# Float64 weights become float32 by one whole-number addition: a change to the conversion and to the order of the first steps of a two-layer float32 kernel

## The chip, the cores and the metric

One NeuronCore of a Trainium2 chip runs the kernel. The metric is the device time of one execution in microseconds, the median of several runs.

## What is computed

```python
def _attn_ref(x, state):                       # x (4, 8, 512, 64), state (4, 8, 32, 64)
    a = softmax(x @ state.T / 8);  xread = a @ state
    a2 = softmax(state @ x.T / 8); sread = a2 @ x
    return np.concatenate([xread, sread], axis=2)

x = attn_out.transpose(0, 2, 1, 3).reshape(4 * 544, 512)   # 2176 tokens
x = (x @ w_a) * (x @ w_b) @ w_out                          # w_a, w_b (512, 1536), w_out (1536, 512)
h = x @ w_in                                               # w_in (512, 2048)
out = (np.maximum(h, 0) + np.log1p(np.exp(-np.abs(h)))) @ w_out2   # w_out2 (2048, 512)
```

(The three lines on the softmax are shortened: the reference subtracts the row's largest score and adds 1e-9 to the sum.) x and state are float32. The five weight matrices are float64, and so are the arithmetic of the last three lines' inputs: each weight arrives in memory as two 32-bit words, low and high.

## The kernel before, in words

**Weights.** A weight unit is loaded as 32-bit words (`load`, `load_first`) and made into float32 on the chip by `convert_to` (line 607). There are 32 units of 128 x 1024 values, which `convert` and `fetch` handle, and four half-units of 128 x 512 (`bring_first`), the two column halves of the first 256 columns of w_a and of w_b, which the start needs. `convert_to` takes six steps on a unit: an activation on ACT that turns the high word, read as a float32, into the upper part with its exponent moved by 2^-112 (helper line 483); a shift by three bits on DVE (line 504); the sign put back (line 508); an AND that keeps sign and exponent (line 504); the low word times 2^-52 times that (line 508); and the float addition of both (line 498).

**Products.** Most products are exact float32 products made of three products of rounded (fp32r) operands. `split_to` (line 577) makes the two operands: a copy to the rounded type, which the planner gives to ACT or DVE (lines 490, 491), and the subtraction of the rest on DVE (line 498). `Products.one` (line 545) issues one product and `turn` (line 560) a transpose on PE.

**Stages.** The first layer is worked in six stages of 256 columns (w_a and w_b) by four batches b. For the first stage the reading of the state is not projected token by token: `state_w` projects the state through w_a and w_b, and the gates are products of attention weights with that. In later stages the same is done by `state_rows` (stage s, half p): it splits a weight unit, makes twelve products of 64 state rows with 512 columns into two pairs of PSUM banks, splits each pair by `split_to`, and copies the rows into place by eight 128 KB DMAs. `gates_of` multiplies the two gate halves, `y_part` multiplies them by w_out and adds up on DVE, `read_x` and `read_y` do the same for the state's own tokens. The second layer follows, with `softplus` between its two products.

**The order.** Nothing runs when the code says it; the code lists steps in a `Plan` with the engines that can do each. `ORDER` (lines 157 to 189) gives the rank of the first 771 steps by number, the rest follows in the program's order. `Plan.go` then walks a modelled time, gives each free engine the ready step of the lowest rank, and takes storage for its results: 36 slots of 128 x 512 in SF, 58 in SR (plus x's own tiles, xf and xr, when x has been used), and 8 PSUM banks of 512 columns. So the table decides the order of the instructions on each engine's queue, and semaphores do the rest. In the first 60 us of its modelled time it puts products of zeros on PE where PE would stand still (line 572).

Of the kernel before, what the change touches and what calls it, by code (L numbers as in the profile page):

```python
# [12 lines left out]
AF = mybir.ActivationFunctionType  # L13
ALU = mybir.AluOpType
# [105 lines left out]
def made(x):  # L120
    return x.ap() if isinstance(x, Ref) else x
# [32 lines left out]


ORDER = """
1 0 3-4 6 18 5 7 17 30 10 19 13 29 20 8 31 22 9 32 21 33 12 23 214 34 11 24 215 14 35 59 25
# [4 lines left out]
118 104 146 106 173 185 147 107 186 119 183 174 236 120 184 190 175 233 121 187 122-123 237  # L162
176 188 150 189 124 158 234 258 191 259 125 247 177-178 162 159 179 192 163 193 260 160 248
261 194 149 151 238 168 165 195 161 264 219 196 201 249 164 218 166 105 240 152 197 167 265
154 182 180 155 153 235 198 220 304 250 181 170 199 171 227 207 262 200 202 239 251 290-291
263 335 252-254 242 228 241 208 221 306 203 307 224 204 223 209 222 225 293 305 210 243 205
255 206 169 244 256 309 266 308 245 294 232 336 211 267 310 229 257 270 311 337 268-269 230
212 246 296 275 213 297 322 321 338 271 226 312 272-274 339 298 276-277 313 315 340 379 314
278 284 341 299 350 316-318 343 300 319-320 279 380 342 371 351 302 324 468 280 325 285 292
301 281 344-345 352 148 372 282 353 469 373 303 382 295 358 286 381 354 374 287 357 327 385  # L170
288 329 355 386 328 470 331 347 383 356 360 346 384 330 323 471 417 333 361 363 387 348 472
366 375 473 407-408 231 401 364 477 367 289 326 332 349 475 418 283 334 376 410 402 478 474
404 359 362 476 498 479-482 365 483 409 405 499 377 388 411 368 378 415 500 462 369 505 403
370 501 406 392 446 433 432 502 506 389 412 438 390 413 439 503 419 393 414 395 435-436 396
441 463 391 504 586 464 442 434 587 448 536 588 449 537 440 451 423 443 420 428 397 444 421
589 445 590 422 452 429 465 579 425 437 484 430 416 485 595 585 431 487 591 596 399 398 488
507 426 454-455 394 427 450 447 457 453 594 490 400 597 491 424 466 510-511 494 512-513
598-599 516-518 458 519 493 526 486 527 529 467 530 523 600 524 520 489 460 508 534 461 509
495 538 496 616 541-543 615 514 497 547 551 532 580 593 552 521 554 456 581 555 622 539 560
617 563 561 531 557 565 623 558 568 533 569 571 573 572 574 583 525 540 546 515 618 566 582  # L180
703 556 492 619 528 559 553 522 562 535 575 459 564 620 545 621 592 601-602 548 604-605
607-608 577 610-611 640 567 576 584 570 654 578 549 544 550 704-705 629 609 733 624 603 606
627-628 630 709 706-707 634-635 651 637-638 708 612-613 643-644 625 646-647 614 712 669 626
641 653 713 671 642 658-661 668 714 655 664-667 645 672 639 715 675 674 677 734 633 678 716
710 631 735 682-683 686 685 739 691 688-689 649 717 692-693 696 648 632 656 736 699 676
701-702 680 650 670 737-738 657 770 652 711 694-695 662-663 673 679 718-732 697 684 681 687
636 740 690 698 741-769 700
"""


# [206 lines left out]
def attention_moe_moe2(ctx, tc, x, state, w_a, w_b, w_out, w_in, w_out2, out):  # L397
# [23 lines left out]
    scale = 1.0 / float(D) ** 0.5  # L421
# [58 lines left out]
    def activation(o, i, func, **kw):  # L480
        also = [v for v in kw.values() if isinstance(v, Ref)]
        acc = [kw["accum_out"]] if "accum_out" in kw else []
        give = lambda: nc.scalar.activation(  # L483
            made(o), made(i), func, **{k: made(v) for k, v in kw.items()})
        plan.add({"act": (act_us(cols(o), in_psum(i)), give)}, [i, *also], [o, *acc])
# [121 lines left out]
    def convert_to(v, b, spare=0):  # L607

        words = b.rearrange("p a b -> p (a b)").bitcast(U32)
        words = words.rearrange("p (c t) -> p c t", t=2)  # L610
        low, high = words[:, :, 0], words[:, :, 1]
        e = Buf(F, v.n, spare)
        v_, e_ = (i.rearrange("p a b -> p (a b)") for i in (v, e.all()))
        vu, eu = v_.bitcast(U32), e_.bitcast(U32)
        activation(v_, high.bitcast(F32), AF.Copy, scale=2.0 ** -112)
        ts(vu, vu, 3, ALU.logical_shift_left)
        stt(vu, high, 0x80000000, vu, ALU.bitwise_and, ALU.bitwise_or)
        ts(eu, vu, 0xFF800000, ALU.bitwise_and)
        stt(e_, low, 2.0 ** -52, e_, ALU.mult, ALU.mult)
        tt(v_, v_, e_, ALU.add)  # L620


    RAW_SPARE = 10
# [735 lines left out]
```

## Time and profile before

| | before |
|---|---|
| median of 3 runs | 735.59 us (735.43 to 736.33) |
| profiled execution: its own time | 734.75 us |
| its span, first to last instruction | 733.0 us |
| mean granted TensorE clock | 0.999 |
| PE busy, matmuls | 726.5 us, 99% |
| PE weight loads (beside the matmuls) | 602.4 us, 82% |
| DVE busy | 608.2 us, 83%, 810 instructions |
| ACT busy | 398.8 us, 54%, 643 instructions |
| HBM read and written | 40.11 MB and 4.46 MB |

The busy time of PE covers pipelined products, each of which starts before the one before it has ended, so a full PE starts a product of 512 columns about every quarter of a microsecond, while one product lasts 0.39 us by itself. DVE and ACT work one instruction after another. In the views "idle before" names what ended the time in which an engine stood still.

### The profile page before, as it was taken

To read this page: it belongs to the slowest core of one execution; us is meant where nothing else is said; L and a number is where in the kernel's file an instruction comes from. 1 tells how busy PE (TensorE), PEld (TensorE's weight loads), DVE (VectorE), ACT (ScalarE), POOL (GpSimd) and SP (SyncE) were. 2 spreads that over 40 slices of the span, in tenths; PEclk is the share of its full clock that TensorE was granted. 3 is DMA by queue.
4 is the path that set the end of the run, shared out by engine and by line. 5 is a ranking of instruction groups with operands and counts; after the bars stand their busy time and mean duration, and the time that the engine had idled before them with its cause. 6 is when DMAs were issued, how large, how long until landed. Compare 5 with 4: busy or idle time off the path is not lost.

```text
span 733.0 us, 10298 instructions
## 1 busy us (share of the span) xinstructions
PE 726.5 (99%) x4090; PEld 602.4 (82%) x4090; DVE 608.2 (83%) x810; ACT 398.8 (54%) x643; POOL 0.7 (0%) x6
## 2 busy tenths in 40 slices
PE   9999999999999999999999999999999999999998
PEld 8577887778888877888888898888988889888897
DVE  7999999999597779799998778569887998886574
ACT  6878655234142323235685676654766657655570
POOL 0000000000000000000000000000000000000000
PEclk9999999999999999999999999999999999999999
DMA  9403791864546356733030001001020110101103
GB/s 308 168 1 130 214 242 48 210 172 107 145 114 173 73 158 149 197 114 116 1 114 1 1 0 59 1 0 58 1 93 24 58 31 28 59 0 59 58 1 129
DMA packets 35379, 66.20 MB, mean 90 GB/s; under 512 B 3716, under 2 KB 10116, under 8 KB 35332
## 3 DMA queue, kind: packets, MB, share of 16 engines
q1 hardware_dynamic: 35332, 65.55, 30.9%
q8 instruction: 32, 0.52, 0.3%
q14 instruction: 15, 0.12, 0.1%
HBM read 40.11 MB, written 4.46 MB: 61 GB/s over the span
## 4 chain that ended last, share of the span: by engine, by line
PE 95%; DVE 2%; ACT 2%; DMA 1%; issue 0%; SPq 0%; ACTq 0%
PE PS L545 93%; PE PS L560 2%; ACT SF L490 1%; ACT SF L483 1%; DVE SF L508 1%; DMA SF<-in_moe_w_a 1%; DVE SR L498 0%; DVE SF L498 0%; DVE SF L504 0%; DVE SM L514 0%; ACT SR L490 0%; SPq L525 0%; DVE SM L519 0%; DVE SM L504 0%; DVE SF L491 0%
## 5 line engine op out<-in xcount | busy, mean ns | idle before, releaser
L545 PE MATMUL PS<-SR 128*128 128x512 f32 (+3 forms) x2187 | 534.5, 377 | 1.2 <-DVE SR L662 1.2
L545 PEld LDWEIGHTS PS<-SR 128*128 128x128 f32 (+1 forms) x2187 | 386.2, 189 | 72.1 <-issue 2.2
L483 ACT ACTIVATE SF<-SF 128x512 f32<-128x512 f32 (+3 forms) x258 | 159.2, 629 | 23.9 <-DMA SF<-in_moe_w_b 10.6
L545 PE MATMUL PS<-SR,xr 128*128 128x512 f32 (+3 forms) x473 | 147.7, 386 | 0.0
L545 PE MATMUL PS<-xr,SR 128*128 128x512 f32 (+1 forms) x378 | 133.1, 391 | 0.0
L490 ACT CAST SR<-SF 128x1024 fp32r<-128x1024 f32 (+4 forms) x97 | 74.6, 772 | 106.4 <-DVE SF L498 104.8
L498 DVE TENSOR_TENSOR SF<-SF,PS 128x1024 f32<-128x1024 f32 (+3 forms) x118 | 108.7, 931 | 26.3 <-PE PS L545 25.5
L508 DVE SCALAR_TENSOR_TENSOR SF<-SF 128x512 f32<-128x512 f32 (+6 forms) x128 | 106.4, 834 | 0.8
L545 PEld LDWEIGHTS PS<-SR,xr 128*128 128x128 f32 x473 | 88.2, 188 | 18.2 <-issue 0.7
L498 DVE TENSOR_TENSOR SR<-SF,SR 128x1024 fp32r<-128x1024 f32 (+4 forms) x96 | 82.2, 862 | 16.1 <-ACT SR L490 15.5
L490 ACT COPY SF<-PS 128x1024 f32<-128x1024 f32 (+3 forms) x88 | 55.5, 663 | 56.4 <-PE PS L545 50.8
L545 PEld LDWEIGHTS PS<-xr,SR 128*128 128x128 f32 (+1 forms) x378 | 68.6, 187 | 15.1 <-issue 0.7
L508 DVE SCALAR_TENSOR_TENSOR SF<-PS,SF 128x512 f32<-128x512 f32 (+2 forms) x74 | 45.1, 609 | 43.1 <-ACT SF L483 43.0
L498 DVE TENSOR_TENSOR SF<-SF 128x512 f32<-128x512 f32 (+3 forms) x103 | 78.2, 761 | 1.6
L483 ACT ACTIVATE SF<-PS 128x512 f32<-128x512 f32 (+2 forms) x78 | 41.5, 532 | 39.7 <-PE PS L545 38.4
L504 DVE TENSOR_SCALAR SF<-SF 128x1024 uint32<-128x1024 uint32 (+1 forms) x61 | 39.4, 652 | 5.8 <-ACT SF L483 5.4
L545 PE MATMUL PS<-SF 64*32 64x128 f32 (+4 forms) x512 | 32.4, 321 | 1.5 <-issue 0.7
L490 ACT CAST SR<-PS 128x1024 fp32r<-128x1024 f32 (+2 forms) x27 | 22.9, 864 | 20.1 <-PE PS L545 11.2
L490 ACT CAST xr<-SF 128x1024 fp32r<-128x1024 f32 (+3 forms) x26 | 20.1, 772 | 25.0 <-DVE SF L498 24.9
L498 DVE TENSOR_TENSOR SR<-PS,SR 128x1024 fp32r<-128x1024 f32 (+2 forms) x29 | 30.1, 1043 | 1.6 <-ACT SR L490 1.3
L545 PEld LDWEIGHTS PS<-SF 64*32 64x32 f32 (+2 forms) x512 | 19.8, 127 | 10.0 <-issue 7.5
L545 PE MATMUL PS<-xr,xr 128*128 128x512 f32 x56 | 22.0, 396 | 0.0
(65 smaller groups left out, 292.1 us busy)
## 6 DMA issues: line engine op xcount, KB each, us to landing
SR<-SR SPq DMA_DIRECT2D x116, 128.0 KB, 2.4
SF<-in_moe_w_out SPq DMA_DIRECT2D x11, 1024.0 KB, 5.0
SF<-in_moe_w_in SPq DMA_DIRECT2D x7, 1024.0 KB, 5.2
SF<-in_moe_w_a SPq DMA_DIRECT2D x11, 512.0 KB, 4.6
SF<-in_moe_w_b SPq DMA_DIRECT2D x11, 512.0 KB, 6.1
xr<-SR SPq DMA_DIRECT2D x36, 128.0 KB, 2.4
x<-in_x SPq DMA_DIRECT2D x8, 512.0 KB, 9.1
out<-SF SPq DMA_DIRECT2D x14, 256.0 KB, 2.2
```

The lines of the kernel that those rows point to most:

```text
L483: give = lambda: nc.scalar.activation(made(o), made(i), func, **{k: made(v) for k, v in kw.items()})
L490: "act": (act_us(n, ps), lambda: nc.scalar.copy(made(o), made(i))),
L498: put = lambda eng: lambda: eng.tensor_tensor(out=made(o), in0=made(a), in1=made(b), op=op)
L504: give = lambda: nc.vector.tensor_scalar(made(o), made(i), s1, None, op0=op0)
L508: give = lambda: nc.vector.scalar_tensor_tensor(out=made(o), in0=made(a), scalar=s, in1=made(b), op0=op0, op1=op1)
L545: self.all.append(lambda: nc.tensor.matmul(made(o), made(w), made(x), start=first, stop=last, **kw))
L560: self.all.append(lambda: nc.tensor.transpose(made(o), made(i), ident))
```

## The change

`convert_to` has five steps instead of six. The upper part is made as before. The low word is multiplied by 2^-29 on ACT and written as a whole number, which rounds it to the bits that the float32 has room for; a 32-bit whole-number addition on DVE adds it to the bits of the upper part. The AND and the product with 2^-52 are gone. `ORDER` is listed anew and covers 1921 steps instead of 771. The helper that issues products of zeros is unchanged.

```diff
 ORDER = """
-1 0 3-4 6 18 5 7 17 30 10 19 13 29 20 8 31 22 9 32 21 33 12 23 214 34 11 24 215 14 35 59 25
...
+0 3-4 6-7 5 1-2 10 8 17 13 9 18-19 29 12 20 11 30 21 31 22 32 207 33 25 23 208 58 34 24 16
...
         activation(v_, high.bitcast(F32), AF.Copy, scale=2.0 ** -112)
+        activation(eu, low, AF.Copy, scale=2.0 ** -29)
         ts(vu, vu, 3, ALU.logical_shift_left)
         stt(vu, high, 0x80000000, vu, ALU.bitwise_and, ALU.bitwise_or)
-        ts(eu, vu, 0xFF800000, ALU.bitwise_and)
-        stt(e_, low, 2.0 ** -52, e_, ALU.mult, ALU.mult)
-        tt(v_, v_, e_, ALU.add)
+        tt(vu, vu, eu, ALU.add)
```

All in all DVE's queue has 55 instructions fewer than before, ACT's 19 more, and PE's 8 fewer, all of them products of zeros. The numbers of lines in the changed kernel lie three higher from `Plan` to `convert_to` (line 545 is 548 there, 498 is 501).

In the rows of the order that follow, PS is PSUM, SR and SF are the two storages, xr_... is x's storage used as SR, and [waits ...] names the engines or DMA queues whose semaphores an instruction waits for.

PE, before: the second of the two blocks of `state_rows` of stage 3 (twelve products, in two lots of six that wait for DVE) stands between products of other work. The first block stands 108 products ahead.

```order
L545 MATMUL PS<-xr_1021,SR 128x512
L545 MATMUL PS<-SR 128x512 x2
L545 MATMUL PS<-xr_1021,SR 128x512
L545 MATMUL PS<-SR 128x512
L545 MATMUL PS<-SR 128x512 [waits DVE_49]
L545 MATMUL PS<-SR 128x512 x5
L545 MATMUL PS<-SR 128x512 [waits DVE_49]
L545 MATMUL PS<-SR 128x512 x5
L545 MATMUL PS<-xr_1021,SR 128x512
L545 MATMUL PS<-SR 128x512
```

PE, with the change: the second half of the first block, the six products of `read_y`, two turns of `read_x`, and the second block, whose halves wait for DVE each.

```order
L548 MATMUL PS<-SR 128x512 [waits DVE_49]
L548 MATMUL PS<-SR 128x512 x5
L548 MATMUL PS<-SR,xr_921 128x512 [waits DVE_49]
L548 MATMUL PS<-xr_880,xr_921 128x512
L548 MATMUL PS<-SR,xr_921 128x512 x2
L548 MATMUL PS<-xr_880,xr_921 128x512
L548 MATMUL PS<-SR,xr_921 128x512
L563 MATMUL PS<-ident,SF 128x128 [waits DMAHW5_49]
L563 MATMUL PS<-ident,SF 128x128
L548 MATMUL PS<-SR 128x512 [waits DVE_49]
L548 MATMUL PS<-SR 128x512 x5
L548 MATMUL PS<-SR 128x512 [waits DVE_49]
```

ACT, with the change, at the same place: the copies of bank pairs to rounded form. The first waits for PE, the second for DVE.

```order
L486 ACTIVATE xf<-SF 128x1024 [waits DMAHW7_49]
L493 CAST SR<-SF 128x1024 [waits DVE_49,PE_49]
L493 CAST SR<-PS 128x1024 [waits PE_49]
L493 CAST SR<-PS 128x1024 [waits DMAHW1_49,DMAHW0_49,DMAHW2_49,DVE_49,Activation_49]
L493 CAST xr_921<-PS 128x256 [waits DVE_49,PE_49]
```

The blocks moved together: about a hundred products stood between them, and eight do now.

DVE, before, at the second block of stage 4: the steps of a conversion and the evictions of banks take turns. On PE eighteen full products stand between that block and the next that waits for one of its banks.

```order
L504 TENSOR_SCALAR SF<-SF 128x1024 [waits Activation_49]
L508 SCALAR_TENSOR_TENSOR SF<-SF 128x1024 [waits DMAHW1_49,DMAHW0_49,DVE_49]
L498 TENSOR_TENSOR SF<-SF,PS 128x1024 [waits PE_49]
L504 TENSOR_SCALAR SF<-SF 128x1024 [waits DVE_49]
L498 TENSOR_TENSOR SR<-PS,SR 128x1024 [waits DMAHW5_49,DMAHW4_49,DMAHW6_49,DMAHW3_49,DMAHW7_49,DMAHW2_49,Activation_49]
L508 SCALAR_TENSOR_TENSOR SF<-SF 128x1024 [waits DVE_49]
L498 TENSOR_TENSOR SR<-PS,SR 128x1024 [waits DMAHW6_49,DMAHW5_49,DMAHW7_49,DMAHW4_49,Activation_49]
```

DVE, with the change, at the first block of stage 4: additions that wait for PE's y products, one conversion of a unit to its end (ISA is the whole-number addition), then the subtractions that free two pairs of banks.

```order
L501 TENSOR_TENSOR SF<-SF,PS 128x1024 [waits PE_49] x4
L507 TENSOR_SCALAR xf<-xf 128x1024 [waits Activation_49]
L511 SCALAR_TENSOR_TENSOR xf<-SF,xf 128x1024 [waits DMAHW7_49,DVE_49]
L501 ISA xf<-xf 128x2048 [waits DVE_49]
L501 TENSOR_TENSOR SR<-PS,SR 128x1024 [waits DMAHW6_49,DMAHW1_49,DMAHW7_49,DMAHW0_49,Activation_49]
L501 TENSOR_TENSOR SR<-PS,SR 128x1024 [waits DMAHW4_49,DMAHW3_49,DMAHW5_49,DMAHW2_49,Activation_49]
```

PE, with the change, there: the last of the y products, the block, and three lots of gate products; the last three wait for the first of those subtractions.

```order
L548 MATMUL PS<-xr_956,xr_880 128x512
L548 MATMUL PS<-SR 128x512 [waits DVE_49]
L548 MATMUL PS<-SR 128x512 x5
L548 MATMUL PS<-SR 128x512 [waits DVE_49]
L548 MATMUL PS<-SR 128x512 x5
L548 MATMUL PS<-SR 128x512 [waits DMAHW1_49,DMAHW0_49,DVE_49]
L548 MATMUL PS<-SR 128x512 x2
L548 MATMUL PS<-SR,xr_921 128x512 [waits DMAHW6_49,DMAHW7_49,DMAHW3_49,DMAHW2_49]
L548 MATMUL PS<-SR,xr_921 128x512 x2
L548 MATMUL PS<-SR,xr_880 128x512 [waits DVE_49]
```

The evictions moved behind a whole conversion, and the products that want their banks moved up: six full products stand between the block and the one that waits.

At the second block of stage 4 DVE now has these rows: its own copy of a bank pair waits for PE's last y product, and an addition and the subtraction follow. On PE the two turns and the block stand right behind that y product, and the block's second half and the gates after it wait for DVE.

```order
L501 TENSOR_TENSOR SF<-SF,PS 128x1024 [waits PE_49] x2
L494 CAST xr_880<-PS 128x1024 [waits PE_49]
L501 TENSOR_TENSOR SF<-SF,PS 128x1024
L501 TENSOR_TENSOR xr_880<-PS,xr_880 128x1024 [waits DVE_49]
L501 TENSOR_TENSOR xr_921<-PS,xr_921 128x256 [waits Activation_49]
```

The rows of before for this block are those of DVE above: the copy was made on ACT there, and the block came 114 products later.

## Rows read from the trace of the kernel before

**Rows 1.** The page: busy time of each engine, and the chain that ended last.
```profile
PE 726.5 (99%) x4090; PEld 602.4 (82%) x4090; DVE 608.2 (83%) x810; ACT 398.8 (54%) x643; POOL 0.7 (0%) x6
...
PE 95%; DVE 2%; ACT 2%; DMA 1%; issue 0%; SPq 0%; ACTq 0%
```

**Rows 2.** Waits of PE: total us, times, longest us; the first three rows.
```profile
PE PS L545 <- DVE SR L662: 1.2, 1, 1.2
PE PS L545 <- issue: 0.7, 1, 0.7
PE PS L545 <- DVE SR L498: 0.5, 1, 0.5
```

**Rows 3.** Windows: length; busy us of PE, PEld, DVE, ACT, POOL; clock; DMA share; GB/s.
```profile
20.00:40.00 20.00, 18.36 (x266) 12.47 (x265) 19.25 (x31) 15.13 (x26) 0.00 (x0) 1.00 0.35 120
40.00:60.00 20.00, 19.90 (x183) 13.44 (x182) 19.84 (x25) 17.32 (x30) 0.00 (x0) 1.00 0.05 9
150.00:250.00 100.00, 100.00 (x461) 80.76 (x460) 82.46 (x80) 33.27 (x35) 0.00 (x0) 1.00 0.55 137
```

**Rows 4.** Groups by line and shape, conversion steps: busy us, mean ns; idle before.
```profile
L483 ACT ACTIVATE SF<-SF 128x512 f32<-128x512 f32 x145 | 91.5, 634 | 5.9 <-DMA SF<-in_moe_w_a 1.0 <-DVE SF L498 0.6 <-DMA SF<-in_moe_w_b 0.5
...
L504 DVE TENSOR_SCALAR SF<-SF 128x1024 uint32<-128x1024 uint32 x53 | 36.1, 687 | 3.9 <-ACT SF L483 3.6
...
L498 DVE TENSOR_TENSOR SF<-SF 128x1024 f32<-128x1024 f32 x25 | 30.5, 1219 | 0.2
L483 ACT ACTIVATE SF<-SF 128x1024 f32<-128x1024 f32 x26 | 29.5, 1136 | 16.6 <-DMA SF<-in_moe_w_b 10.1 <-DMA SF<-in_moe_w_out 6.5
...
L508 DVE SCALAR_TENSOR_TENSOR SF<-SF 128x1024 f32<-128x1024 uint32 x23 | 28.1, 1223 | 0.4
L508 DVE SCALAR_TENSOR_TENSOR SF<-SF 128x1024 uint32<-128x1024 uint32 x23 | 28.1, 1223 | 0.3
```

**Rows 5.** Timeline of DVE, first conversion: start us, length us, instruction.
```profile
6.87 0.43 DVE L504 TENSOR_SCALAR SF<-SF 128x512 uint32<-128x512 uint32 x1
7.34 0.69 DVE L508 SCALAR_TENSOR_TENSOR SF<-SF 128x512 f32<-128x512 uint32 x1
8.06 0.69 DVE L498 TENSOR_TENSOR SF<-SF 128x512 f32<-128x512 f32 x1
```

**Rows 6.** Timeline of PE from 19.61 us; idle time before in brackets.
```profile
19.61 1.97 PE L560 MATMUL PS<-ident,x 128*128 128x128 f32 x16
21.97 0.66 PE L560 MATMUL PS<-ident,SF 128*128 128x128 f32 x4 [0.39 <-ACT SF L490]
22.38 0.71 PE L572 MATMUL PS<-SR 128*128 128x256 f32 x4
23.02 1.44 PE L545 MATMUL PS<-SF 64*32 64x128 f32 x64
...
27.45 0.69 PE L545 MATMUL PS<-SF 64*32 64x128 f32 x29 [0.50 <-DVE SR L498]
28.88 3.62 PE L545 MATMUL PS<-SF 64*32 64x128 f32 x41 [0.74 <-issue]
```

**Rows 7.** The chain that ended last: start us, length us, what.
```profile
63.90 9.55 PE PS L545 x42
```

**Rows 8.** Groups by line and shape, evictions of PSUM: columns as in rows 4.
```profile
L498 DVE TENSOR_TENSOR SF<-SF,PS 128x1024 f32<-128x1024 f32 x59 | 71.6, 1216 | 16.9 <-PE PS L545 16.5
...
L498 DVE TENSOR_TENSOR SR<-PS,SR 128x1024 fp32r<-128x1024 f32 x21 | 25.4, 1218 | 1.3 <-ACT SR L490 1.3
...
L490 ACT CAST SR<-PS 128x1024 fp32r<-128x1024 f32 x19 | 18.9, 1016 | 15.6 <-PE PS L545 10.4 <-DMA xr<-SR 2.2 <-PE PS L560 1.6
```

**Rows 9.** Timeline of PE at a block of `state_rows`, stage 4.
```profile
202.80 0.38 PE L560 MATMUL PS<-ident,SF 128*128 128x128 f32 x2
203.11 1.65 PE L545 MATMUL PS<-SR 64*128 64x512 f32 x12
204.69 0.97 PE L545 MATMUL PS<-SR,xr 128*128 128x512 f32 x3
```

More of the change, by code (lines that the diff above doesn't have):

```diff
@@ L156 @@
 ORDER = """
-1 0 3-4 6 18 5 7 17 30 10 19 13 29 20 8 31 22 9 32 21 33 12 23 214 34 11 24 215 14 35 59 25
[4 rows of a table removed]
[L162 to L184, printed above, removed]
@@ L185 @@
-710 631 735 682-683 686 685 739 691 688-689 649 717 692-693 696 648 632 656 736 699 676
-701-702 680 650 670 737-738 657 770 652 711 694-695 662-663 673 679 718-732 697 684 681 687
-636 740 690 698 741-769 700
+0 3-4 6-7 5 1-2 10 8 17 13 9 18-19 29 12 20 11 30 21 31 22 32 207 33 25 23 208 58 34 24 16
+209 59 128 60 36 35 210 129 61 38 26 130 63 62 37 14 67 39 15 28 40 70 27 41 76 71 43 78 87
+45-46 42 64 123 44 47 66 88 80 77 48 124 131-132 68 134 85 121 50 133 54 51 49 86 73 135 122
[3 rows of a table added]
+252 143 154 182 230 155 183 169 253 226 188 119 254 170 227 211 189 171-173 240 156 120 212
@@ new lines @@
+158 241 144 157 297 257 174 147 159 148 242 255 258 160 298 201 256 101 149 162 192 244 163
+150 176 243 175 259 231 161 245-247 299-300 193 228 195-196 194 233 164-165 260 232 262 202
+328 197 261 301 198-199 236 204 203 302 234-235 200 205 264 213 268 206 263 284 237-238 329
+214 331 283 269 265-267 286 220 215 342 248 216 221 249 239 287 330 223 303 217 315 289 250
+290 332 218 304 343 314 344 291 270 333 305 273 224 285 345 271 292 306-307 274 222 219 309
+293 317 288 308 277 370 279 334 310 346 318 311-312 225 336 335 280 347 272 313 362 364 363
@@ new lines @@
+275 278 376 294 316 371 320 295-296 349 373 324 348 339 374 321 338 351-352 281 337 354 375
+322 357-358 372 487 323 325 486 488-489 355 319 408 490 397 466 398 365 400 327 367 458 407
+391 276 467 392 468 377 405 394-395 340 378 469-470 341 359 401 471 492 459 462 366 572 326
+573 436 461 423 452 460 356 368 523 360 350 369 353 463 574 524 361 399 493 402 393 379 491
+382 403 422 282 381 575 429 380 406 426 577 580 464 385 576 396 453 581 428 454 386-387 409
+582 600 388 583 430 425 437 584 431 585 424 383 432 413 404 601 384 439 410 438 419 434 441
@@ new lines @@
+389 411-412 606 498 455 566 442 435 418 433 607 472 416 473 475-476 390 494 415 521 427 478
[4 rows of a table added]
+552 529 551 571 561 535 696 559 589-590 579 694 592-593 595 562 530 587 608 563 638 531 537
+588 613 564 596 609 556 611-612 614 594 565 557 618-619 624 635 621 560 610 692 627-628 695
+630-631 597 615 653 591 625 598 616 655 632 642-645 622 599 652 648-651 629 656 623 636 659
+639 658 661 717 617 662 555 693 715 718 666-667 670 669 720 675 672-673 633 586 676-677 680
+626 640 716 683 660 685 699 664 634 654 719 641 751 554 687 678-679 646-647 657 663 700-714
@@ L188 @@
+681 668 665 671 620 721 674 682 722-750 684 752-801 803-804 802 805-823 825-826 824 827-851
+853-854 852 855-877 879-880 878 881-966 968-969 967 970-1186 1188-1189 1187 1190-1230
+1232-1233 1231 1234-1247 1249-1250 1248 1251-1283 1285-1286 1284 1287-1503 1505-1506 1504
+1507-1547 1549-1550 1548 1551-1564 1566-1567 1565 1568-1600 1602-1603 1601 1604-1820
+1822-1823 1821 1824-1864 1866-1867 1865 1868-1881 1883-1884 1882 1885-1917 1919-1920 1918
 """
```

11 rows, old and new, of the table ORDER are left out of this document.

## Prediction

> **What bounds the kernel now.** I read the page's busy times and its chain first, then TensorE's waits, then the windows, then the timeline of the places that the change touches. TensorE (PE) is busy for 726.5 of the 733.0 us of the span, and the chain that ended last is 95% PE [rows 1]. PE's list of waits, sorted by size, begins with 1.2 us for the first zeros at the very start, and goes on with 0.7 and 0.5 us [rows 2]. Between 150 and 250 us PE has no idle time at all, 100.00 of 100.00. Only the first 60 us leave something: 18.36 of 20 and 19.90 of 20 us, in the windows from 20 to 60 [rows 3]. So work taken from VectorE (DVE) or given to ScalarE (ACT) is worth nothing by its sum. It is worth what it does to the first 60 us, and what it does to the moment at which a PSUM bank that PE wants comes free.
>
> **Part 1, the six steps that become five.** For a unit of 1024 columns the AND (0.687 us) and the product with 2^-52 (1.223 us) go, and the float addition (1.219 us) becomes a whole-number addition; for a unit of 512 columns 0.43 and 0.69 us go [rows 4, 5]. There are 32 units of the first kind and four of the second: 32 x 1.91 + 4 x 1.12 = 65.6 us less on DVE. ACT gets one more activation per unit, 1.136 or 0.634 us [rows 4]: 32 x 1.136 + 4 x 0.634 = 38.9 us. ACT is busy 54% of the span and DVE 83% [rows 1]; both lie beside a PE that is full, so both sums go into the result as nothing. The cover is the distance between a unit's load and its first product. Where it ends, it ends in a wait for a bank, and those are in part 3.
>
> The whole-number addition has no row. The instruction order shows it as one instruction over 2048 columns for a unit of 1024 words, so over 16-bit halves. From below: 0.687 us, the row of a 1024-column step with one input [rows 4]. From above: if it goes through 2048 columns at the pace of the float addition, which takes 0.69 us for 512 [rows 5] and 1.219 for 1024 [rows 4], that is 1.219 + 2 x 0.53 = 2.28 us. I take 1.22 us, the float addition's row, because it reads two inputs and moves the same number of bytes. The Trainium skill, page "VectorE: DVE Perf Modes", section "The perf-mode tier table", puts a 16-bit tensor_tensor over 2,048 columns at 1224 ns and a 4-byte float one at 2293 ns: by the first figure the sum here stays as it is, by the second it is that of the third rival below. No row here shows either.
>
> **Part 2, the start.** The first conversion runs on DVE without a gap: the steps that go are the AND, at 6.87 us, and the product with 2^-52, at 7.34 us; the addition follows at 8.06 us [rows 5]. Four of these half-units lie one behind the other before the first gate products, which need the state projections of all four. Four times 1.12 us is 4.5 us of DVE. PE cannot use all of it, since the last of x that the start needs lands at 19.7 us whatever DVE does: PE's turns of x begin at 19.61 us and run without a wait [rows 6]. After them PE waits 0.39, 0.50 and 0.74 us, and fills 0.64 us (22.38 to 23.02) with zero products [rows 6]. That is 2.27 us which a DVE that is 4.5 us further on can give back. From below it is nothing, if the waits only move to the next turn; from above 2.4 us, the 1.74 us that PE is idle from 20 to 60 us [rows 3] and the 0.64 us of zero products. I take **2.0 us gained**, near the top, as DVE's relief is twice what PE can use. Eight zero products fewer are issued in the whole program; they only stand in waits and give nothing of their own. In SyncE's queue the second half of w_b moves from the ninth to the eighth load, and the second half of x's third batch is the eleventh in both, so the landing that holds PE at 19.6 us is not moved.
>
> **Part 3, the three waits that come.** The list of first steps is new, and in it the blocks that project the state rows through the next stage's weights (twelve products of 64 rows) stand closer together and closer to other products. A block takes two pairs of banks of the four pairs there are, and a pair is free only when its values are copied to rounded form and subtracted (the copy takes 1.016 us on ACT, and on DVE as I take it 1.22, like the addition from PSUM; the subtraction 1.218 on DVE [rows 8]). PE's side of each sum uses 0.227 us per full product (9.55 us for 42 [rows 7]), 1.58 us for a block (203.11 to 204.69) and 0.31 us for two turns (202.80 to 203.11) [rows 9].
>
> *Stage 3, near 159 us.* Before, its two blocks stand 108 products apart. Now six products and two turns lie between them. ACT's first copy waits for PE, because it writes into slots that the first block still reads. From the end of that block: copy 1.02, subtract 1.22, then the next copy 1.02 and subtract 1.22, since the second copy waits for DVE: 4.48 us until the second pair of banks is free. PE has six products (1.36), two turns (0.31) and half of the second block (0.79) to do meanwhile: 2.46. PE waits **2.0 us** in two pieces. If ACT's first copy could start before the block ends, 1.0 us less.
>
> *Stage 4, first block, near 188 us.* The bank that the second group of gate products wants belongs to an older pair, and its subtraction now stands on DVE behind an addition that waits for the end of PE's y products, a shift, a sign step and the whole-number addition of one weight unit. From the end of the y products: 1.22 + 0.69 + 1.22 + 1.22 + 1.22 = 5.57 us [rows 4, 8]. PE has the block (1.58) and six products (1.36): 2.94. PE waits **2.6 us**, or 2.1 if the whole-number addition takes 0.69 us. Behind the waiting subtraction stand another subtraction and the split of a weight unit, which come later by as much as PE does.
>
> *Stage 4, second block, near 214 us.* DVE itself makes a rounded copy that waits for PE's last y product, and behind it stand an addition and the subtraction. Each of the last two frees a bank pair that PE wants: 1.22 + 1.22 + 1.22 = 3.66 us. PE has two turns and the block, 0.31 + 1.58 = 1.89. PE waits **1.8 us**. Before, this block comes over 100 products later, and eighteen full products lie between it and the first that wants one of its banks.
>
> **The sum.** -2.0 + 2.0 + 2.6 + 1.8 = +4.4 us. It stands against the profiled execution, 734.75 us: 739.2 us. The median of the runs lies 0.84 us above that execution (735.59), so I expect 740.0 us as the median. The ends: with the start at -2.4 and the waits at 4.4 us in all (stage 3 with 1.0, the whole-number addition at 0.69 us, half a us off the last) it is 737.6. With no gain in the start and 8.5 us of waits (each subtraction late by another 0.7 us, as some of them also wait for 128 KB copies of state rows) it is 744.1.
>
> **The rivals.**
> *Faster: the banks come free in time.* Then only the start is left: 734.75 - 2.0 + 0.84 = 733.6 us. For it speaks that DVE has 66 us less to do, and that before the largest wait of PE for DVE, the first zeros apart, is 0.5 us [rows 2]. Against it, the queues of DVE and ACT are served in the order shown, and each of the three chains begins at an event of PE, so that being early elsewhere doesn't shorten it. It decides if each chain is about 2 us shorter than I count. Chance 0.12.
> *No change.* The start gives 2.4 us, and the waits come to about as much, since two of the three are covered: within 1.5 us of 735.6. Chance 0.08.
> *Slower still: the whole-number addition takes 2.28 us.* Its price is 1.06 us per unit and 0.53 per half-unit. The start loses 4 x 0.53 = 2.1 us of what it gained, and the wait near 188 us grows by 1.06: 740.0 + 2.1 + 1.06 = 743.2 us at least. The other 31 units would add up to 33 us on DVE, of which a part would reach PE; I put this case at 745 or more. It is also the case in which the addition isn't the cheap step that the change counts on. Chance 0.06.
>
> **How the numbers follow.** The forecast, three new waits that outweigh the start, has 0.74; its own range is 737.6 to 744.1, and its time is 740.0. A change under 0.2% (1.5 us) is about what a measurement of this kernel can't tell from none. Faster is the first rival, 0.12; same is the second, 0.08; slower is the forecast and the third, 0.80. The range goes from 736.0 to 744.1: below it stays the first rival, above it most of the third, under 0.2 together.
>
> **What would show it.** In the profile of the changed kernel, the stretch of PE that begins at 28.88 us [rows 6] should begin near 26.9. PE's waits should have three new places: about 2 us near 159, 2.6 near 188 and 1.8 near 214 us, each put down to DVE. The windows from 150 to 250 us should have 6 us of idle PE, and after 300 us nothing should change. The whole-number addition should show 1.2 us, DVE some 543 us busy and ACT some 438. I am wrong if PE is busy throughout from 150 to 250 us (first rival), or if the addition's row shows 2.3 us (third).

## The result, and the profile after

The changed kernel takes 742.3 us, the median of six runs (740.72 to 744.86). The kernel before took 735.51 us (735.31 to 736.33), measured beside it. The ratio is 1.0094, with an interval from 1.0073 to 1.0115, so the change made the kernel slower by nearly 7 us. The forecast was 740.0 us, with a range from 736.0 to 744.1. The profiled execution took 741.0 us. Its span is 739.1 us, which is 6.1 us more than before.

The page, and after it the first rows of PE's waits, answer to [rows 1, 2]. Line numbers are three higher than before, behind `convert_to` two.

```profile
PE 727.4 (98%) x4082; PEld 602.3 (81%) x4082; DVE 561.9 (76%) x755; ACT 422.1 (57%) x662; POOL 0.7 (0%) x6
...
PE 91%; DMA 4%; DVE 3%; ACT 1%; issue 0%; SPq 0%; ACTq 0%
```

```profile
PE PS L548 <- DVE SR L501: 3.8, 4, 2.4
PE PS L548 <- DVE SF L501: 1.3, 1, 1.3
PE PS L548 <- DVE SR L664: 1.2, 1, 1.2
PE PS L548 <- issue: 1.1, 1, 1.1
PE PS L563 <- DVE SF L511: 1.0, 1, 1.0
```

DVE is busy for 46 us less and ACT for 23 us more, and the kernel is slower. The list of waits says why: PE's longest wait for DVE, the first zeros apart, was 0.5 us before and is 2.4 us now.

The windows (columns as in [rows 3]) show where PE stands idle.

```profile
20.00:40.00 20.00, 18.86 (x284) 13.48 (x269) 19.09 (x31) 19.71 (x33) 0.00 (x0) 1.00 0.34 119
40.00:60.00 20.00, 20.00 (x205) 13.89 (x206) 19.69 (x25) 17.18 (x30) 0.00 (x0) 1.00 0.19 64
...
150.00:200.00 50.00, 46.50 (x215) 35.88 (x214) 29.51 (x29) 17.00 (x18) 0.00 (x0) 1.00 0.40 105
200.00:250.00 50.00, 48.50 (x219) 39.31 (x218) 34.31 (x33) 17.05 (x18) 0.00 (x0) 1.00 0.66 153
```

From 150 to 250 us PE had no idle time before; now it has 3.50 + 1.50 = 5.0 us. The timelines of PE and DVE at the first block of stage 4 show the longest wait as it arises. The columns are start, length, instruction, and in brackets the idle time before it.

```profile
187.70 2.55 PE L548 MATMUL PS<-SR 64*128 64x512 f32 x15
190.08 0.85 PE L548 MATMUL PS<-SR,xr 128*128 128x512 f32 x3
193.34 0.97 PE L548 MATMUL PS<-SR,xr 128*128 128x512 f32 x3 [2.40 <-DVE SR L501]
```

```profile
187.81 1.22 DVE L501 TENSOR_TENSOR SF<-SF,PS 128x1024 f32<-128x1024 f32 x1 [1.50 <-PE PS L548]
188.95 0.69 DVE L507 TENSOR_SCALAR xf<-xf 128x1024 uint32<-128x1024 uint32 x1
189.67 1.23 DVE L511 SCALAR_TENSOR_TENSOR xf<-SF,xf 128x1024 uint32<-128x1024 uint32 x1
190.93 1.22 DVE L501 CUSTOM_DVE_ANT_0 xf<-xf 128x2048 uint16<-128x2048 uint16 x1
192.07 2.35 DVE L501 TENSOR_TENSOR SR<-PS,SR 128x1024 fp32r<-128x1024 f32 x2
```

The first of the two subtractions in the last row frees the bank that the products at 193.34 want. It comes after an addition that waited for PE and after the last three steps of one conversion. Nothing in those three steps concerns PE at that moment.

**Where the 6.1 us are.** The same work is compared, not the same time. A block of state rows begins at 124.68 us before and at 125.19 us now, but six more full products stand ahead of it now (6 x 0.227 = 1.36 us). So the start gained 0.85 us. A later block, of stage 5, has the same useful products ahead of it in both and begins at 270.93 and at 276.38, 5.45 us later; the stretch between the two blocks therefore lost 6.3 us. The last product of the program is 6.10 us later, so another 0.65 us was lost after that. In sum: -0.85 + 6.3 + 0.65 = 6.1. These are single executions: in the first two kernels below that move steps of stage 4 and share this start, the block of state rows begins at 125.17 and 125.60 us, so the 0.85 has some 0.4 us of play.

### The profile page after: what moved, and what is told of

The parts are those of the page before. It is cut to its first block, busy times and chain, and to the rows that moved or that the text cites. A ratio compares the mean times of both kernels' runs of the same rounds, so it can differ in the third digit from the quotient of the medians.

```text
span 739.1 us, 10278 instructions
## 1 busy us (share of the span) xinstructions
PE 727.4 (98%) x4082; PEld 602.3 (81%) x4082; DVE 561.9 (76%) x755; ACT 422.1 (57%) x662; POOL 0.7 (0%) x6
## 4 chain that ended last, share of the span: by engine, by line
PE 91%; DMA 4%; DVE 3%; ACT 1%; issue 0%; SPq 0%; ACTq 0%
PE PS L548 89%; DMA SF<-in_moe_w_b 2%; PE PS L563 2%; DMA SR<-SR 1%; DVE SR L501 1%; DMA SF<-in_moe_w_a 1%; DVE SF L501 1%; ACT SF L493 0%; DVE SM L517 0%; ACT SF L486 0%; DVE SR L494 0%; DVE SF L494 0%; SPq L528 0%; DVE SF L511 0%; DVE xr L501 0%
## 5 line engine op out<-in xcount | busy, mean ns | idle before, releaser
L548 PE MATMUL PS<-SR 128*128 128x512 f32 (+3 forms) x1980 | 489.9, 379 | 4.2 <-DVE SR L501 1.4
L548 PEld LDWEIGHTS PS<-SR 128*128 128x128 f32 (+1 forms) x1980 | 348.2, 189 | 72.6 <-issue 2.9
L548 PE MATMUL PS<-SR,xr 128*128 128x512 f32 (+2 forms) x580 | 165.4, 379 | 2.4 <-DVE SR L501 2.4
L548 PE MATMUL PS<-xr,SR 128*128 128x512 f32 (+2 forms) x452 | 151.3, 388 | 0.0
L486 ACT ACTIVATE SF<-SF 128x512 f32<-128x512 f32 (+5 forms) x191 | 135.4, 725 | 20.9 <-DMA SF<-in_moe_w_b 10.3
L548 PEld LDWEIGHTS PS<-SR,xr 128*128 128x128 f32 x580 | 106.4, 188 | 23.1 <-DVE SR L501 2.8
L511 DVE SCALAR_TENSOR_TENSOR SF<-SF 128x1024 uint32<-128x1024 uint32 (+4 forms) x61 | 52.4, 859 | 0.3
L501 DVE CUSTOM_DVE_ANT_0 SF<-SF 128x2048 uint16<-128x2048 uint16 (+1 forms) x33 | 38.1, 1155 | 1.6
L486 ACT ACTIVATE SF<-xf 128x512 f32<-128x512 f32 (+4 forms) x53 | 34.8, 662 | 5.6 <-DMA xf<-in_moe_w_out 4.6
L548 PE MATMUL PS<-SF 64*32 64x128 f32 (+4 forms) x512 | 32.2, 321 | 1.1 <-issue 1.1
L486 ACT ACTIVATE xf<-SF 128x512 f32<-128x512 f32 (+4 forms) x46 | 29.6, 648 | 3.1 <-DMA SF<-in_moe_w_out 1.3
```

The source lines that it names most:

```text
L486: give = lambda: nc.scalar.activation(made(o), made(i), func, **{k: made(v) for k, v in kw.items()})
L501: put = lambda eng: lambda: eng.tensor_tensor(out=made(o), in0=made(a), in1=made(b), op=op)
L511: give = lambda: nc.vector.scalar_tensor_tensor(out=made(o), in0=made(a), scalar=s, in1=made(b), op0=op0, op1=op1)
L548: self.all.append(lambda: nc.tensor.matmul(made(o), made(w), made(x), start=first, stop=last, **kw))
```

## The experiments

Nine kernels were run. The medians of the kernel before, run beside them, lie between 735.45 and 735.94 us. My theory was that a few evictions that stand behind other work on DVE's queue cost the time, and that the arithmetic of the conversion costs none. The first rival was that the new list of steps is to blame as a whole, the second that the conversion is.

**One half of the change alone.** The table `ORDER` and the steps of `convert_to` can be exchanged separately, if the numbers in a list are carried over to the same steps. The first kernel has the new conversion with the old list:

```diff
 ORDER = """
-0 3-4 6-7 5 1-2 10 8 17 13 9 18-19 29 12 20 11 30 21 31 22 32 207 33 25 23 208 58 34 24 16
+1 0 3-4 6 18 5 7 17 31 10 19 13 29 20 8 32 22 9 30 21 12 23 207 33 11 24 208 14 34 58 25 60
...
```

> The new conversion, with the list of first steps of the kernel before (each step keeps its place; the activation of the low word takes the place of the AND, the product with 2^-52 is dropped). Theory, the list makes the loss: the waits of 2.4 us near 191 us and 1.3 near 218 us are gone, PE's idle time from 150 to 250 us is under 1.5 us, and the time is 735 to 738 us. Rival, the conversion itself makes the loss (39 us more on ACT, the whole-number addition in a chain): the time stays at 740 to 743 us, whatever the order.

It took 740.33 us (739.29 to 741.58; ratio 1.0068, 1.0053 to 1.0083), about 2 us less than the changed kernel. The two long waits were gone and PE was idle for 1.46 us from 150 to 250 us, as my theory had it, but the time is the rival's. The second has the old conversion with the new list (against the changed kernel; the list is the same but for its numbers, and is not shown):

```diff
-        activation(eu, low, AF.Copy, scale=2.0 ** -29)
         ts(vu, vu, 3, ALU.logical_shift_left)
         stt(vu, high, 0x80000000, vu, ALU.bitwise_and, ALU.bitwise_or)
-        tt(vu, vu, eu, ALU.add)
+        ts(eu, vu, 0xFF800000, ALU.bitwise_and)
+        stt(e_, low, 2.0 ** -52, e_, ALU.mult, ALU.mult)
+        tt(v_, v_, e_, ALU.add)
```

> The six conversion steps of the kernel before, with the changed kernel's list of first steps (the AND and the product with 2^-52 stand right behind the sign step, the low word's activation is dropped). Theory, the list makes the loss: waits of 1 to 3 us at blocks of state rows between 120 and 250 us, over 4 us of idle PE there, and 741 to 748 us, since DVE has 66 us more to do in the same list. Rival, the conversion makes the loss: 734.5 to 736.5 us, as the kernel before.

It took 748.52 us (747.53 to 749.31; ratio 1.0176, 1.0159 to 1.0193), the slowest median of all and half a microsecond above what my theory gave; the time of its rival is out. The four combinations are:

| median, us | old list | new list |
|---|---|---|
| six steps | 735.5 | 748.5 |
| five steps | 740.3 | 742.3 |

With the new list the five steps are 6 us faster than the six; with the old list they are 5 us slower. So neither part has a price of its own. That a list fits the steps that it stands beside, and loses when they change, is how I read the four numbers; they alone do not show it. In the kernel with the old list the waits stand elsewhere: PE loses 1.79 us from 100 to 150 us, where the changed kernel loses 0.06.

```profile
100.00:150.00 50.00, 48.21 (x220) 37.99 (x220) 40.55 (x41) 25.36 (x28) 0.00 (x0) 1.00 0.61 178
150.00:200.00 50.00, 48.64 (x223) 38.39 (x222) 33.33 (x32) 13.75 (x16) 0.00 (x0) 1.00 0.42 97
```

**Three steps moved.** From here on the placement is held: the plan of the changed kernel is walked once, the queue that comes out is edited, and only then are the instructions issued. In the first edit the shift, the sign step and the whole-number addition of one unit go behind the first of the two subtractions near 192 us:

```diff
+MOVES = [
+    (689, 'behind', 533),
+    (690, 'behind', 689),
+    (691, 'behind', 690),
+]
...
```

> The changed kernel with every instruction, slot and bank as it was, but three DVE instructions of one conversion (shift, sign step, whole-number addition of the unit of w_out of stage 4) stand behind the subtraction that frees the bank, instead of ahead of it. Theory, queueing on DVE makes the wait near 191 us: PE's wait there goes from 2.4 us to under 0.3 and everything behind it comes earlier by 2.3 to 2.9 us, so the time falls by as much, to about 739.7 us; the waits near 163 and 218 us stay. Rival, the bank is held by something else (DMA of state rows, ACT's copy): the wait stays over 1.5 us and the time within 1 us of the changed kernel's.

The median is 740.46 us (738.49 to 742.15; ratio 1.0068, 1.0048 to 1.0088). The profiled execution took 738.49 us, its span is 736.4 us, 2.7 us less than in the changed kernel. On PE and on DVE the place now reads as follows (line numbers are higher, since lines were added):

```profile
187.75 2.55 PE L569 MATMUL PS<-SR 64*128 64x512 f32 x15
190.14 1.53 PE L569 MATMUL PS<-SR,xr 128*128 128x512 f32 x6
```

```profile
187.86 1.22 DVE L522 TENSOR_TENSOR SF<-SF,PS 128x1024 f32<-128x1024 f32 x1 [1.50 <-PE PS L569]
189.00 1.22 DVE L522 TENSOR_TENSOR SR<-PS,SR 128x1024 fp32r<-128x1024 f32 x1
```

The subtraction begins 3.07 us earlier and PE goes on without a gap. From the block at 187.70 and 187.75 us to the block of stage 5 PE takes 88.68 us in the changed kernel and 85.94 here (to 273.69), so the 2.7 us lie in this stretch. No instruction was taken away; the gain came from three places in one queue. This shows the mechanism for the largest of the waits. The medians differ by less, 1.8 us, and the runs of the two kernels overlap.

**One copy more on ACT.** At the second block of stage 4 DVE makes a rounded copy that the old kernel made on ACT. This kernel gives it back to ACT, beside the three moves:

```diff
     (691, 'behind', 690),
+    (615, 'act', 0),
 ]
```

> As the kernel before this one, and the rounded copy of a bank pair near 217 us is made by ACT instead of DVE, in the same place of the order. Theory: ACT's copy (1.02 us) runs beside the addition, the wait near 218 us falls from 1.5 us in all to 0.4 to 0.9, and the time by 0.8 to 1.2 us more, to about 738.7 us. Rival, ACT is held there by its own queue: no change beyond 0.3 us against the run with the three steps moved alone.

The median is 742.35 us (742.21 to 744.36; ratio 1.0101, 1.0086 to 1.0116), worse than without the copy's move, which neither my theory nor its rival gave. The wait near 218 us did fall, from 1.33 + 0.17 to 0.20 + 0.16 us. But another came at 244 us, here on PE and then on DVE:

```profile
244.36 0.50 PE L570 MATMUL PS<-SR 128*128 128x512 f32 x1 [2.59 <-DVE SF L523]
```

```profile
242.48 0.69 DVE L529 TENSOR_SCALAR SF<-SF 128x1024 uint32<-128x1024 uint32 x1 [6.47 <-ACT SF L508]
243.09 1.21 DVE L523 TENSOR_TENSOR SF<-SF,PS 128x1024 f32<-128x1024 f32 x1
```

A shift of the next conversion stands ahead of the addition that frees PE's bank. DVE stood still for 6.47 us ahead of it, as the unit's load had landed later than in the kernel without the move: ACT begins on the unit at 241.33 us, and at 238.84 there. Why it landed later is not shown. The windows behind that wait show something more; it is the last section's.

**More moves.** Five more edits of the same kind, beside the three moves (eight in all, where the expectation counts nine): the copy on ACT, a shift and a sign step behind the addition that frees the bank near 244 us, a sign step of the start behind a copy of scores, and a shift of the second layer behind a subtraction.

```diff
     (691, 'behind', 690),
+    (615, 'act', 0),
+    (717, 'behind', 623),
+    (718, 'behind', 717),
+    (107, 'behind', 90),
+    (879, 'behind', 761),
 ]
```

> The changed kernel with its slots and banks as they were, and nine changes of place, each of a DVE or ACT instruction that stood ahead of one that frees a bank PE waits for: the three behind the subtraction (near 191 us) and the copy on ACT (near 218), as before, and the shift and sign step of the second unit of w_a and w_b of stage 5 behind two additions (near 241, where in the run with the copy on ACT they waited for their load and PE waited 2.6 us behind them), the sign step of the first unit of w_out behind a copy (near 27), a shift of a unit of w_in behind a subtraction (near 301). Theory, the loss of the changed kernel is what stands ahead of evictions in the queues of DVE and ACT: PE keeps only the waits of the start and some 1.1 us near 163; span 733 to 735 us and time 735 to 737.5, so level with the kernel before or within 2 us of it. Rival, each wait removed comes back at the next place where PE and DVE meet: 738 us or more.

The median is 737.92 us (737.00 to 739.91; ratio 1.0037, 1.0023 to 1.0051). The median lies just above the range of my theory and just below the rival's. So 4.4 of the 6.8 us come back by eight edits that remove no work. What PE still waits for, besides the start, is stage 3 (0.33 and 0.77 us of the first row), 0.62 us at 297.62 and small change.

```profile
PE PS L574 <- DVE SR L527: 1.7, 3, 0.8
PE PS L589 <- DVE SF L537: 1.4, 1, 1.4
```

No version that I ran is faster than the kernel before; this one comes nearest.

**The start.** The forecast counted 2.0 us for it and 0.85 came. Two kernels take work out of it, with the placement held; both leave out the low words of the first 256 columns of w_a and w_b. The first takes some 2 us from ACT: the low word of the half-units is made in eight of its 512 columns, and a float addition of the upper part to itself stands in for the whole-number addition.

```diff
-        activation(eu, low, AF.Copy, scale=2.0 ** -29)
+        half = v.n == 1
+        activation(eu, low, AF.Copy, scale=2.0 ** -29, some=8 if half else None)
...
-        tt(vu, vu, eu, ALU.add)
+        tt(*((v_, v_, e_) if half else (vu, vu, eu)), ALU.add, twice=half)
```

> The changed kernel in its order; in the four half-units of the start the activation of the low word writes 8 columns instead of 512, and the addition adds the upper part to itself as floats in the same time, so the low words of the first 256 columns of w_a and w_b are left out. ACT has some 2.0 us less to do before 30 us, DVE as much as before. Theory, ACT took over what DVE gave back in the start (ACT is busy for 19.7 of the 20 us from 20 to 40): the block of state rows that begins at 125.2 us in the changed kernel begins 1 to 2 us earlier. Rival, a chain of dependences (softmax and state reads) bounds the start, and no single engine's work: under 0.5 us earlier.

The second takes some 2 us from DVE: the addition of the half-units is made in eight columns.

```diff
-        tt(vu, vu, eu, ALU.add)
+        tt(vu, vu, eu, ALU.add, some=8 if v.n == 1 else None)
```

> The changed kernel in its order; in the four half-units of the start the whole-number addition adds 8 columns instead of 512, so the low words of the first 256 columns of w_a and w_b are left out; ACT has as much to do as before, DVE some 2.2 us less before 20 us. Theory, DVE no longer bounds the start: the block of state rows that begins at 125.2 us in the changed kernel begins less than 0.5 us earlier. Rival, DVE still bounds it: 1 to 2 us earlier.

The block that begins at 125.19 us in the changed kernel began at 125.33 and at 125.30, with the same products ahead. Single executions took 742.84 and 741.19 us. So neither less ACT work nor still less DVE work brought the block forward. The second is the weaker test. Its execution ran at half the granted clock for a while in the start, as its windows show (the clock is the third column from the right):

```profile
18.00:20.00 2.00, 2.00 (x18) 1.94 (x17) 1.98 (x4) 1.59 (x3) 0.00 (x0) 0.57 1.06 400
20.00:22.00 2.00, 2.00 (x23) 0.86 (x22) 1.18 (x3) 1.24 (x2) 0.00 (x0) 0.58 1.03 363
```

PE was 1.35 us behind the changed kernel at 23.96 us and 0.14 behind it at 31.12: a pause of PE near 28.5 us, to which the account of part 2 comes back, hid the loss. The two kernels that follow put work back. In the first the half-units are converted by the six old steps, which shifts the numbers of the list by sixteen:

```diff
-        activation(eu, low, AF.Copy, scale=2.0 ** -29)
+        if v.n > 1:
+            activation(eu, low, AF.Copy, scale=2.0 ** -29)
...
-        tt(vu, vu, eu, ALU.add)
+        if v.n > 1:
+            tt(vu, vu, eu, ALU.add)
+            return
+        ts(eu, vu, 0xFF800000, ALU.bitwise_and)
+        stt(e_, low, 2.0 ** -52, e_, ALU.mult, ALU.mult)
+        tt(v_, v_, e_, ALU.add)
```

> The four half-units of the start (512 columns) are converted by the six old steps, the 32 units of 1024 by the five new ones; the new list, with its numbers shifted to the sixteen more steps. This puts 4 x 1.12 = 4.5 us of DVE work back into the start. Theory A (the start is not bound by DVE's amount of work, so the change gained next to nothing there): the first block of state rows after 100 us begins within 0.5 us of the 125.2 us of the changed kernel, once the useful products ahead of it are counted. Rival A (the start did gain about 2 us from the shorter conversion, and lost it elsewhere): it begins 1.5 us or more later. Theory B (where the list puts evictions against products is chance as soon as the steps differ from those that it was listed for): sixteen steps more in the first few us shift every later placement, so that the waits near 163, 191 and 218 us go or change places, with a median between 736 and 745 that no sum over the steps gives. Rival B (the waits belong to the list's own order): all three stay at their blocks with 1.1, 2.4 and 1.5 us, and the median stays within 1 us of 742.3 or is the start's loss above it.

The block began at 127.34 us with the same useful products ahead, 2.15 us later: theory A missed and rival A was met. The three waits near 163, 191 and 218 us were gone altogether, as theory B had it, and one of 2.63 us stood at 214. The median was 741.9 us (741.28 to 744.89; ratio 1.0097, 1.0072 to 1.0122). Since this kernel's list is shifted too, the last one holds the placement and puts two steps without effect on DVE ahead of each of the four additions:

```diff
+                if more:
+                    eng.tensor_scalar(made(b), made(b), 0xFFFFFFFF, None, op0=ALU.bitwise_and)
+                    eng.scalar_tensor_tensor(
+                        out=made(b), in0=made(b), scalar=0, in1=made(b),
+                        op0=ALU.bitwise_and, op1=ALU.bitwise_or)
                 eng.tensor_tensor(out=made(o), in0=made(a), in1=made(b), op=op)
...
-        tt(vu, vu, eu, ALU.add)
+        tt(vu, vu, eu, ALU.add, more=v.n == 1)
```

> The changed kernel with its placement held, and two steps that change nothing put on DVE ahead of the addition of each of the four half-units of the start: an AND with all ones and an OR with zero, in shape and size the two steps that the change took away there (0.43 and 0.69 us). So DVE's work of the start is that of before, 4.5 us more, and all else stays. Theory A (the shorter conversion of the half-units is worth about 2 us of PE's time, the part of it that PE could use, and the new order of the start gave some of it back): the first block of state rows after 100 us begins near 127.3, about 2 us later than in the changed kernel (125.2), and the median is near 744. Rival (it is worth nothing, and the 2.2 us seen with the old half-units came from the shifted list): the block begins within 0.5 us of 125.2, and the median is within 1 us of 742.3.

The first of the four conversions shows the two steps at 0.42 and 0.69 us (timeline of DVE):

```profile
8.53 0.42 DVE L520 TENSOR_SCALAR SF<-SF 128x512 uint32<-128x512 uint32 x1
8.99 0.69 DVE L521 SCALAR_TENSOR_TENSOR SF<-SF 128x512 uint32<-128x512 uint32 x1
9.71 0.69 DVE L524 CUSTOM_DVE_ANT_0 SF<-SF 128x1024 uint16<-128x1024 uint16 x1
```

The block began at 129.59 us, 4.40 us later. Of that 1.3 us is not the edit's: in this execution the first conversion begins 1.30 us later than in the changed kernel (7.46 against 6.16), as ACT got its first weights later, and the first turn of x waited 1.9 us for its load. That leaves 3.1 us. The median is 745.78 us (744.11 to 747.74; ratio 1.0125, 1.0090 to 1.0159): two runs took 744.1 us, 3.1 above the changed kernel's profiled execution, and two 747.4 and 747.7, the profiled one among them. So the rival is out; the theory's direction came, with a larger size. The 4.5 us of DVE that the change takes out of the start are worth some 2 us (by the kernel with the old half-units) to 3 us of PE (by this one, less its late load), and no gain was seen from a further 2 us.

## Why the prediction was right, and where its sizes were off

The forecast case came in: the three waits came, at the three blocks that the order pointed to, each put down to DVE, and they outweighed the start. The time lies 2.3 us above the forecast and inside its range. That the sum came so near is in part luck: a start that gave too little and two losses that were not forecast add up to the difference, and the 6.4 us of waits match the 6.3 us lost in that stretch although only 5.0 of them are idle time.

**Part 1 held.** The step without a row, the whole-number addition, takes 1.22 us, the value taken. Here are the groups by shape (columns as in [rows 4]):

```profile
L501 DVE CUSTOM_DVE_ANT_0 SF<-SF 128x2048 uint16<-128x2048 uint16 x29 | 35.4, 1220 | 1.3
...
L486 ACT ACTIVATE SF<-SF 128x1024 uint32<-128x1024 uint32 x25 | 28.7, 1147 | 2.6 <-DMA SF<-in_moe_w_b 2.6
```

So the third rival (2.28 us) is out. The Trainium skill's figure for a 16-bit tensor_tensor over 2,048 columns (page "VectorE: DVE Perf Modes", section "The perf-mode tier table", 1224 ns) agrees with this row's 1220 ns, though the page gives it for bf16 and the row is of whole numbers. DVE fell by 46 us and not by 66, and ACT rose by 23 and not by 39: the new list also has DVE make rounded copies that ACT made before (of one such shape 19 stood on ACT in [rows 8], and 15 do now). In all DVE makes 50 copies of one kind or another, 17 more than before, and ACT 17 fewer; on DVE they add up to 10.9 us. I had moved only the conversion's steps between the engines.

**Part 3 held in place and mechanism.** Idle time was forecast at 2.0, 2.6 and 1.8 us; it is 0.33 + 0.76, 2.40 and 1.33 + 0.17 us, 5.0 together against 6.4. In each of the five pieces PE also waits out the end of its last product, which costs 0.39 - 0.227 = 0.16 us more: 5.8 us. By the comparison of the same work above, the stretch lost 6.3. The half us between them I could not place. The chain at 188 us ran as it was worked out, step for step, and the experiment with three steps moved took it away. The one at 163 us was shorter than forecast. Here are PE and ACT there:

```profile
162.78 0.96 PE L548 MATMUL PS<-SR 64*128 64x512 f32 x6 [0.33 <-DVE SR L501]
164.50 1.85 PE L548 MATMUL PS<-SR 64*128 64x512 f32 x9 [0.76 <-DVE SR L501]
```

```profile
160.45 1.02 ACT L493 CAST SR<-PS 128x1024 fp32r<-128x1024 f32 x1 [4.43 <-PE PS L548]
162.18 1.01 ACT L493 CAST SR<-PS 128x1024 fp32r<-128x1024 f32 x1 [0.71 <-DMA SR<-SR]
```

I had the second copy wait for DVE's subtraction. It waited 0.71 us, and by the trace for a DMA of state rows, so copy and subtraction overlap in part. The chain from the end of the block to the second pair of banks is 160.57 to 164.50, 3.9 us, where I had 4.48.

**Part 2 failed in its size.** "Near the top, as DVE's relief is twice what PE can use" gave 2.0 us; 0.85 came. The reason behind it was sound: with DVE's old amount of work the block lies 2.15 us and about 3.1 us later in the last two experiments, by the last even more than I allowed. Two things were wrong beside it. I left out that the same new list also reorders the start: with the old amount of work the new order lies 1.3 us (2.15 - 0.85) to some 2.2 us (3.1 - 0.85) behind the kernel before. And of the 2.27 us that I let DVE give back, the largest wait, 0.74 us, is put down to "issue" in [rows 6] and not to DVE. Two pauses stand in the start now that were not there in this size before:

```profile
15.76 1.06 PE L563 MATMUL PS<-ident,x 128*128 128x128 f32 x8 [0.97 <-DVE SF L511]
...
28.52 2.61 PE L548 MATMUL PS<-SF 64*32 64x128 f32 x31 [1.09 <-issue]
```

The second answers to the pause that ended at 28.88 us before [rows 6]. I expected its end near 26.9; it ended at 28.52. It stands inside a run of like products. Counted from the start of the program it stands behind the 475th product, before and after alike, as windows that end in the pause show (before first; the counts of products and of weight loads stand in brackets):

```profile
0.00:28.50 28.50, 25.42 (x475) 21.67 (x476) 22.82 (x44) 21.42 (x35) 0.70 (x6) 1.00 0.91 305
0.00:28.20 28.20, 25.23 (x475) 22.43 (x476) 21.73 (x40) 22.17 (x37) 0.70 (x6) 1.00 0.92 309
```

Six of the other kernels pause behind their 475th product too: the one with the old list, the three with moved steps, and the two with less work in the start. In these eight traces the pause ends between 28.40 and 28.93 us: at 28.60 with less ACT work in the start, and at 28.67 with less DVE work, where PE came late and paused only 0.27 us. In each of them a load of 16 KB on the DMA queue of kind "instruction" lands 1.2 to 1.6 us before that end (at 27.18 us in the changed kernel, at 27.51 before). The other three reach that product only at 32.2 us or later and do not pause there. So the pause goes with a place in the program and not with DVE's work. PE reached it 0.7 us earlier than before, its end moved by 0.35 us, and the pause grew from 0.74 to 1.09 us. That PE waits there for the code of its program would fit; no run moved the pause, so this is not shown.

**Two things were not forecast.** After 300 us nothing was to change, but behind the block at 276.38 us 0.65 us were lost, about half of it a wait for DVE (0.33 us at 300.81). And the median lies 1.3 us above the profiled execution, where I took 0.84 us: among the timed runs, the two longest, 744.05 and 744.86 us, have a mean granted clock of 0.995, and the three shortest (740.72, 741.00 and 741.81 us) have 0.999.

## What to carry to other kernels

Beside an engine that was busy 99% of the time, less work on its helpers was worth nothing by its sum; what counted was what stood ahead of the one instruction that frees a bank. So before a step is made cheaper, read for each wait of the full engine which instruction releases it, and follow the releasing engine's queue back to the last event of the full engine: that sum, less the work that the full engine has meanwhile, gave 2.6 us where 2.40 were measured. Leave out of a gain what the view puts down to no engine (here "issue"): a faster helper did not move it. And a list of ranks may have to be fitted again, or edited by hand at the long waits, when steps go or come: both lists here lost some 5 to 6 us beside the other steps.

## What the runs showed of the hardware that I had not expected

The granted clock fell after some of PE's waits, and not after others. In the kernel with the copy on ACT, the windows behind the wait of 2.59 us show it (the clock is the third column from the right):

```profile
242.00:244.00 2.00, 0.00 (x0) 0.00 (x0) 1.52 (x2) 1.48 (x2) 0.00 (x0) 1.00 0.69 162
244.00:246.00 2.00, 1.64 (x6) 1.32 (x7) 2.00 (x3) 1.05 (x1) 0.00 (x0) 0.82 0.22 51
246.00:248.00 2.00, 2.00 (x6) 1.58 (x5) 2.00 (x3) 1.01 (x1) 0.00 (x0) 0.50 0.00 0
248.00:250.00 2.00, 2.00 (x9) 1.62 (x8) 1.83 (x2) 1.05 (x1) 0.00 (x0) 0.83 0.00 0
```

0.50 is 1.2 GHz. With 0.72, 2.0 and 0.68 us at that level (a mean of 0.82 over 2 us is 0.72 us at half), it stayed there for some 3.4 us, so PE did 1.7 us less work beside the 2.59 us that it stood still. The same follows a wait of 2.63 us in the kernel with the old half-units (clock 0.50 from 216 to 218 us), and one of 1.96 us in the one with the old steps and the new list (0.50 from 94 to 96 us). But in the changed kernel's profiled execution the wait of 2.40 us at 191 us is followed by a clock of 1.00:

```profile
192.00:194.00 2.00, 0.66 (x3) 0.57 (x4) 2.00 (x3) 1.13 (x1) 0.00 (x0) 1.00 0.02 7
194.00:196.00 2.00, 2.00 (x11) 1.61 (x10) 1.55 (x2) 0.00 (x0) 0.00 (x0) 1.00 0.00 0
```

Two experiments on the start hold the placement of the changed kernel, the one with less ACT work and the one with two steps added on DVE. They have the same wait of 2.40 us at the same block, and there the fall came. With less ACT work the windows behind it are:

```profile
194.00:196.00 2.00, 2.00 (x7) 1.55 (x6) 1.76 (x2) 0.58 (x1) 0.00 (x0) 0.60 0.00 0
196.00:198.00 2.00, 2.00 (x7) 1.54 (x5) 0.00 (x0) 0.00 (x0) 0.00 (x0) 0.55 0.00 0
```

The kernel with less DVE work has that wait too and no fall behind it (1.00 from 192 to 200 us). So the same wait in the same order of instructions is followed by a fall in two executions and by none in two, and its length alone does not say whether the clock falls. The price can be read between two blocks with the same work, the first block of stage 4 and the first of stage 5: 88.68 and 88.71 us without a fall, 90.22 and 90.54 with one, so 1.5 to 1.9 us. The lower mean clock of the longest runs of the changed kernel would fit such falls in some of its executions; their traces were not taken, so for them this is argued and not shown.
